# Filling a wait at a seam: eight early products, one transpose moved, and other shares of filler work

## The chip, the core and the metric

The kernel runs on one core of one Trainium2 chip. The metric is the device time of one execution in microseconds (us); lower is better. Matmuls run on TensorE (PE in the profile, with its weight loads as PEld), element-wise work on VectorE (DVE), exponentials and logarithms on ScalarE (ACT). GpSimd (POOL) and SyncE (SP) mainly start transfers here.

## The reference

Attention over 8 batches of 12 heads, with one extra term in the softmax's denominator, followed by a two-layer network with a squared ReLU over all 3584 tokens:

```python
batch, n_heads, seq, head_dim = (8, 12, 448, 64)
n_tokens, d_model, d_ff = (3584, 768, 2048)

scores = scale * q @ k.T
m = max(scores, axis=-1)
e = exp(scores - m)
attn = e / (sum(e) + exp(-m) + 1e-09)
x = (attn @ v)                 # heads side by side: 3584 x 768
h = x @ w_in                   # 768 x 2048
g = max(h, 0) ** 2
out = g @ w_out                # 2048 x 768, float32
```

The kernel leaves the maximum out of the exponent (sum(exp(s)) + 1 is the same denominator), so a head pair needs scores, exponentials, their sums, the products with v and one multiplication by the reciprocal.

## The kernel before

The order of the instructions on each engine is the order in which the program names them. Work is cut in units: one unit is one head pair of one batch, and unit number i is also the round of the loop that starts it. Batch 0 is cut twice: units 0 to 5 are its six head pairs for queries 0 to 191, units 6 to 11 the same pairs for queries 192 to 447. Units 12 to 17 are batch 1, 18 to 23 batch 2, and so on; from unit 18 on they run three to a cycle.

While a unit's exponentials run on ScalarE, TensorE is kept busy with products of the first layer, which are taken one at a time from a queue:

```python
def tile_in(t0, n, f0, per):          # one tile of the first layer: per * 6 products
    hp = mp_tile()                    # a PSUM tile: the pool m_psum has three
    for j in range(per):
        for dc in range(DCH):         # DCH = 6: the six head pairs are the contraction
            product(hp[...], win[...], xt[:, dc, x0:x0 + n], ...)
            yield n / 2.4             # nominal ns of a product of n columns
    relu_squared(hp, t0, n, f0, per)  # two VectorE instructions: rt, gs (they free hp)

def tiles_in_early(n, f0, per, ready):    # the first two tiles of batch 0
    hps = [mp_tile(), mp_tile()]
    for t, dcs in ((0, range(ready)), (1, range(ready)), (0, range(ready, DCH)), (1, range(ready, DCH))):
        ...     # first the 16 products that need only pairs 0 to 3, then the 8 that need pairs 4 and 5

def drain(ns):
    while ins and ns > 0:
        ns -= one(ins)                # one product; subtracts its nominal ns

def transposes(b, pr):                # q and k of one head pair: 16 transposes and a VectorE copy
    tp = mp_tile(FP16)
    ...                               # 16 x nc.tensor.transpose(tp[...], naturals[...], ident)
    nc.vector.tensor_copy(qks[b][...], tp[...])
```

A product is two matmuls of 64 columns of weights each. All tiles named mp (first layer, sums, transposes) come from the same three PSUM buffers; the values' tile xp has one buffer of its own. From the first cycle on every fourth mp tile takes xp's buffer.

```python
FIRST = 192
transpose_at = {pr - 1: [(0, pr)] for pr in range(1, NPAIR)}       # NPAIR = 6
for i, at in ((10, (1, 0)), (11, (1, 1)), (11, (1, 2)), (13, (1, 3)), (14, (1, 4)), (15, (1, 5)), (16, (2, 0)),
              (17, (2, 1)), (17, (2, 2))):
    transpose_at.setdefault(i, []).append(at)

for i in range(NPAIR, 2 * NPAIR):              # rounds 6 to 11
    u, et, es, half = begin(i)
    two = units[i - 2:i] if i % 2 == 0 else None    # even rounds sum and normalise two units
    if i % 2 or i == NPAIR:
        xp = x_psum.tile(...)
    scores(u, et, 0)                           # 4 matmuls, then one exponential of 112x1024
    if i == NPAIR:                             # the seam: round 6
        sums(i - 1)                            # VectorE: es of unit 5
        values_of(i - 2, xp)
        values_of(i - 1, xp)
        rcp = sums_of(i - 2)                   # TensorE: 4 matmuls; ScalarE: Ln, then Exp(-x)
        normalise(two, xp, rcp)                # VectorE: xt of pairs 4 and 5
        scores(u, et, 1)
        queue(0, FIRST)                        # 8 tiles of 12 products
        share[0] = left() / (NPAIR + 4)
    else:
        for at in transpose_at.get(i, ()):
            transposes(*at)
        drain(16 * FIRST / 2.4 if i == NPAIR + 1 else share[0] * 0.45)
        scores(u, et, 1)
        values_of(i - 1, xp)
        if two:
            rcp = sums_of(i - 2)
        drain(share[0] * 0.3)
    add_chunks(u, et, es, half, 1)             # VectorE: half
    if two and i > NPAIR:
        normalise(two, xp, rcp)
    add_chunks(u, et, es, half, 2)             # VectorE: es
    if i > NPAIR:
        drain(share[0] * 0.25)

for i in range(2 * NPAIR, 3 * NPAIR):          # rounds 12 to 17 (batch 1)
    ...
    scores(u, et, 0)
    for at in transpose_at.get(i, ()):
        transposes(*at)
    drain(share[0] * (1.2 if first else 0.45))
    scores(u, et, 1)
    ...                                        # round 12: values, sums; later rounds: sums, values of unit i - 1
    drain(share[0] * 0.15)
    for step in range(3):
        add_chunks(u, et, es, half, step)      # VectorE: es, half, es
        drain(share[0] * (0.15, 0.1, 0.15)[step])
    if i == 3 * NPAIR - 1:
        run(ins, len(ins))
        rcps[i] = row_sums([u], ...)           # sums of unit 17
    normalise(done, xp, rcp)
    if first:
        queue(FIRST, S - FIRST)                # 8 tiles of 12 products of 256 columns
        share[0] = left() / (NPAIR - 0.2)

for i in range(3 * NPAIR, NU, 3):              # the cycles
    for j in range(3):
        begin(i + j)
        for kk in range(RUN):
            scores(units[i + j], ets[i + j], kk // 2, (kk % 2,))
            ...                                # VectorE sums
            if (j, kk) != (2, RUN - 1):
                rows(5 if (RUN * j + kk) % 3 == 0 else 4)   # second layer: 4 or 5 steps of two matmuls
    ...
    if b in ON_PE and pr == 0:
        for x in range(3):
            transposes(b, 3 + x)
```

Of the kernel before, what the change touches and what calls it, by code (L numbers as in the profile page):

```python
# [15 lines left out]
def kernel(  # L16
# [14 lines left out]
    NPAIR = H // 2  # L31
# [121 lines left out]
    def transposes(b, pr):  # L153
        tp = mp_tile(FP16)
        for i, name in enumerate("qk"):
            for s in range(RUN):
                for h in range(2):
                    nc.tensor.transpose(tp[64 * h:64 * h + 64, i, P * s:P * s + P],  # L158
                                        naturals[name, b, pr][:, h, s, :], ident[0:P, 0:P])
        if b not in qks:  # L160
            qks[b] = qk_pool.tile([128, 3, COLS], FP16, name="qk")
        parts = (0, S // 2, S) if b == 0 and pr < 3 else (0, S)
        for x, y in zip(parts, parts[1:]):
            nc.vector.tensor_copy(qks[b][:, 0:2, pr * S + x:pr * S + y], tp[:, :, x:y])  # L164
# [67 lines left out]
    def values(u, et, xp, o=0):  # L232
        b, pr, _, n = u
        for kk in range(RUN):
            for h in range(2):
                nc.tensor.matmul(xp[64 * h:64 * h + 64, o:o + n], vns[b][:, 2 * pr + h, kk, :],  # L236
                                 of_head(chunk(et, u, kk // 2, kk), u, h), start=(kk == 0), stop=(kk == RUN - 1))

    def row_sums(us, sums):

        n = us[0][3]
        m = n * len(us)
        zp = mp_tile()
        for j, (u, parts) in enumerate(zip(us, sums)):
            for x, es in enumerate(parts):
                total = es[:, 0:2 * n]
                if n < S:
                    total = total.rearrange("p (h n) -> p h n", h=2)
                for h in range(2):
                    nc.tensor.matmul(zp[64 * h:64 * h + 64, j * n:(j + 1) * n], ones, of_head(total, u, h),  # L250
                                     start=(x == 0), stop=(x == len(parts) - 1))
        rcp = z_pool.tile([128, 512], FP32, name="rcp")
        nc.scalar.activation(out=rcp[:, 0:m], in_=zp[:, 0:m], func=AF.Ln, bias=one_b)  # L253
        nc.scalar.activation(out=rcp[:, 0:m], in_=rcp[:, 0:m], func=AF.Exp, scale=-1.0)  # L254
        return rcp
# [14 lines left out]
    def mp_tile(dtype=FP32):  # L270
        if joined[0] >= 0:
            joined[0] += 1
        pool, name = (x_psum, "xp") if joined[0] > 0 and joined[0] % 4 == 0 else (m_psum, "mp")
        return pool.tile([128, 512] if dtype == FP32 else [128, 2, 512], dtype, name=name)
# [22 lines left out]
    def tile_in(t0, n, f0, per):  # L297

        xt, x0 = xts[t0 // S], t0 % S
        hp = mp_tile()  # L300
        for j in range(per):
            fb = f0 + j
            for dc in range(DCH):
                product(hp[:, j * n:(j + 1) * n], win[:, dc, fb * 128:(fb + 1) * 128],
                        xt[:, dc, x0:x0 + n], start=(dc == 0), stop=(dc == DCH - 1))
                if j < per - 1 or dc < DCH - 1:
                    yield n / 2.4
        relu_squared(hp, t0, n, f0, per)
        yield n / 2.4

    def tiles_in_early(n, f0, per, ready):

        xt = xts[0]
        m = per * n
# [3 lines that stand above are left out]
                fb = f0 + per * t + j  # L318
                for dc in dcs:
                    product(hps[t][:, j * n:(j + 1) * n], win[:, dc, fb * 128:(fb + 1) * 128],  # L320
                            xt[:, dc, 0:n], start=(dc == 0 and j == 0), stop=(dc == DCH - 1 and j == per - 1))
                    if dc < DCH - 1 or j < per - 1:
                        yield n / 2.4
            if dcs[-1] == DCH - 1:
                relu_squared(hps[t], 0, n, f0 + per * t, per)
                yield n / 2.4
# [71 lines left out]
    def queue(t0, n):  # L398

        per = max(1, 512 // n)  # L400
        first = 0
        if t0 + n == FIRST:
            first = 2 * per
            ns = first * DCH * n / 2.4
            ins.append([ns, ns, tiles_in_early(n, 0, per, DCH - 2)])
        for f0 in range(first, NFFB, per):
            ns = per * DCH * n / 2.4
            ins.append([ns, ns, tile_in(t0, n, f0, per)])
# [10 lines left out]
    def left():  # L419
        return sum(t[0] for t in ins)  # L420

    def one(tiles):

        got = next(tiles[0][2])
        tiles[0][0] -= got
        if tiles[0][0] < 1.0:
            tiles.pop(0)
        return got

    def drain(ns):  # L430
        while ins and ns > 0:
            ns -= one(ins)
# [6 lines left out]
    FIRST = 192  # L439
# [3 lines left out]

    transpose_at = {pr - 1: [(0, pr)] for pr in range(1, NPAIR)}
    for i, at in ((10, (1, 0)), (11, (1, 1)), (11, (1, 2)), (13, (1, 3)), (14, (1, 4)), (15, (1, 5)), (16, (2, 0)),
                  (17, (2, 1)), (17, (2, 2))):
        transpose_at.setdefault(i, []).append(at)

    def keep_warm(n):
# [4 lines left out]
    share = [0.0]  # L454
# [25 lines left out]
    def sums_of(at):  # L480
        return row_sums(units[at:at + 2], (ess.pop(at)[0:1], ess.pop(at + 1)[0:1]))

    def values_of(at, xp):
        values(units[at], ets.pop(at), xp, at % 2 * units[at][3])
# [38 lines left out]
    for i in range(NPAIR, 2 * NPAIR):  # L523
        u, et, es, half = begin(i)
        two = units[i - 2:i] if i % 2 == 0 else None
        if i % 2 or i == NPAIR:
            xp = x_psum.tile([128, 512], FP32, name="xp")
        mode[0] = COLS2
        scores(u, et, 0)
        if i == NPAIR:  # L530
            sums(i - 1)
            values_of(i - 2, xp)
            values_of(i - 1, xp)
            rcp = sums_of(i - 2)
            normalise(two, xp, rcp)
            scores(u, et, 1)
            queue(0, FIRST)
            share[0] = left() / (NPAIR + 4)
        else:
            for at in transpose_at.get(i, ()):  # L540
                transposes(*at)
            drain(16 * FIRST / 2.4 if i == NPAIR + 1 else share[0] * 0.45)
            scores(u, et, 1)
            values_of(i - 1, xp)
            if two:
                rcp = sums_of(i - 2)
            drain(share[0] * 0.3)
        add_chunks(u, et, es, half, 1)
        if two and i > NPAIR:
            normalise(two, xp, rcp)  # L550
        add_chunks(u, et, es, half, 2)
        if i > NPAIR:
            drain(share[0] * 0.25)
        if i == NPAIR + 5:
            load_natural(2, 0, 3)
            for n0 in (0, HALF):
                for j in range(2):
                    load_wout(n0, j, 2)
# [56 lines left out]
    def add(at, *steps):  # L615
        for step in steps:
            add_chunks(units[at], ets[at], *ess[at], step)
# [5 lines left out]
    for i in range(3 * NPAIR, NU, 3):  # L623
        b, pr = units[i][0:2]
# [4 lines that stand above are left out]
                if kk == 0 and j:  # L629
                    add(i + j - 1, 1, 2)  # L630
                if kk == 1:
                    add(i + j, 0)
                if (j, kk) != (2, RUN - 1):
                    rows(5 if (RUN * j + kk) % 3 == 0 else 4)
        mode[0] = COLS2
        for at in pending:
            take_in(at)
# [3 lines that stand above are left out]
        if pr == 0:  # L641
            queue((b - 1) * S, S)
            if b > 2:
                run(outs)
            if b + 1 < B:
                transposed_loads(b + 1)
                hold(b + 1)
                load_v(b + 1, 0, NPAIR)
                if b + 2 < B:
                    stage(b + 2)  # L650

        run(ins, 1 if pr == 0 else 2)
        add(i + 2, 1)
        run(ins, 1)
        add(i + 2, 2)
        sum_up(i, i + 1)
        run(ins, 2)
        sum_up(i + 2)
        run(ins, 3 if pr == 0 else 4)
        if pr:  # L660
            complete(b * S)
        pending = [i, i + 1, i + 2]
# [36 lines left out]
```

The softmax here doesn't subtract the row's maximum and nothing guards it: scores larger than these inputs give would overflow.

## Time and profile before

| What | Value |
|---|---|
| time, median of 3 runs | 412.65 us (412.32 to 413.08) |
| span of the profiled execution | 410.6 us |
| granted TensorE clock | 0.999 |
| VectorE busy over the span | 289.8 us (71%) |
| ScalarE busy over the span | 234.4 us (57%) |
| TensorE busy, 10 to 20 us | 8.73 us of 10 |
| TensorE busy, 20 to 30 us | 9.18 us of 10 |
| TensorE busy, 65 to 70 us | 3.75 us of 5 |
| TensorE busy, 80 to 140 us | 60 us of 60 |

The span can be read in stages from the starts of the scores on TensorE: rounds 0 to 5 fill the first 17.7 us, round 6 begins at 17.70 us, round 12 at 35.87, round 17 at 59.86, and the first cycle at 67.5 us. [...] consecutive matmuls overlap in the record: what a group costs TensorE is read from the start of the group to the start of the next, not from its duration.

### The profile page before, as it was taken

The numbers are of one execution on the slowest core, as the hardware profiler recorded it, in microseconds if no ns is written. First come the engines' busy times: TensorE is split into PE (matmuls) and PEld (weight loads), VectorE is DVE, ScalarE is ACT, GpSimd is POOL, SyncE is SP. The second block draws the span as 40 slices with busy tenths as digits, with TensorE's granted clock in tenths as the row PEclk, the third lists the DMA queues.
The fourth block names the chain that finished last, engine by engine and source line by source line (L and its number), as shares of the span: only waits on it lengthen the run. The fifth ranks groups of instructions, "written<-read, shape, count | busy, mean of one in ns | idle before, by whom it ended". The sixth has DMA issues, their size and how long they took to land.

```text
span 410.6 us, 10685 instructions
## 1 busy us (share of the span) xinstructions
PE 401.0 (98%) x4715; PEld 259.0 (63%) x4715; DVE 289.8 (71%) x554; ACT 234.4 (57%) x312; POOL 36.3 (9%) x58
## 2 busy tenths in 40 slices
PE   7899998999999999999999999999999999999997
PEld 3577676755576666666566666667566665555664
DVE  3778896978976787777876788867876789186000
ACT  5998997667393745559383755739464663100111
POOL 7524030020000200001000030001000000000000
PEclk9999999999999999999999999999999999999999
DMA  9999999689114891499304992297102010010222
GB/s 203 197 198 197 203 202 219 127 132 219 60 42 107 135 219 25 98 183 182 100 2 114 168 179 64 77 188 124 41 2 69 11 41 2 38 40 0 78 77 78
DMA packets 75823, 45.58 MB, mean 111 GB/s; under 512 B 42560, under 2 KB 72000, under 8 KB 75456
## 3 DMA queue, kind: packets, MB, share of 16 engines
q0 software_dynamic: 28848, 22.16, 35.6%
q1 hardware_dynamic: 46208, 22.05, 23.1%
q8 instruction: 37, 0.61, 0.6%
q10 hardware_dynamic: 720, 0.69, 0.5%
q14 instruction: 10, 0.08, 0.1%
HBM read 45.69 MB, written 17.93 MB: 155 GB/s over the span
## 4 chain that ended last, share of the span: by engine, by line
PE 89%; ACT 4%; DVE 4%; DMA 1%; issue 1%
PE mp L286 24%; PE mp L352 17%; PE mp L288 11%; PE xp L286 8%; PE sp L201 6%; PE xp L352 5%; PE mp L236 5%; PE xp L288 3%; PE xp L236 3%; PE sp L189 3%; ACT et L169 3%; PE mp L250 2%; PE mp L158 1%; DMA et<-in_k_dram 1%; DVE qk L164 1%; ACT rcp L253 1%
## 5 line engine op out<-in xcount | busy, mean ns | idle before, releaser
L169 ACT ACTIVATE et<-sp 112x896 f16<-112x896 f32 (+2 forms) x144 | 125.2, 915 | 40.7 <-PE sp L201 30.6
L352 PE MATMUL mp<-wout,gs 64*128 64x384 f16 x896 | 115.2, 322 | 0.0
L286 PEld LDWEIGHTS <-win 128*64 128x64 f16 x1536 | 83.9, 110 | 45.6 <-issue 1.5
L286 PE MATMUL mp<-xt,win 128*64 128x448 f16 (+2 forms) x1200 | 107.0, 323 | 0.3 <-DVE qk L164 0.2
L293 DVE TENSOR_SCALAR rt<-mp 128x448 f16<-128x448 f32 (+2 forms) x96 | 59.7, 622 | 26.3 <-PE mp L286 13.8
L352 PEld LDWEIGHTS <-gs 64*128 64x128 f16 x1152 | 58.1, 94 | 21.1
L295 DVE TENSOR_TENSOR gs<-rt 128x448 f16<-128x448 f16 (+2 forms) x128 | 50.2, 392 | 4.4
L352 PE MATMUL xp<-wout,gs 64*128 64x384 f16 x256 | 53.1, 323 | 0.0
L253 ACT ACTIVATE rcp<-mp,one_b 128x448 f32<-128x448 f32 (+2 forms) x42 | 26.5, 630 | 41.9 <-PE mp L250 41.7
L361 ACT ACTIVATE ot<-mp 128x384 f32<-128x384 f32 (+1 forms) x16 | 7.6, 477 | 64.5 <-PE mp L288 48.2
L201 PE MATMUL sp<-qk 64*112 64x224 f16 x480 | 43.1, 258 | 0.0
L169 ACT ACTIVATE nn<-sp 112x896 f16<-112x896 f32 x48 | 41.7, 917 | 1.6
L201 PEld LDWEIGHTS <-qk 64*112 64x112 f16 x480 | 30.6, 128 | 14.2 <-issue 3.6
L286 PE MATMUL xp<-xt,win 128*64 128x448 f16 x336 | 36.5, 352 | 0.0
L288 PEld LDWEIGHTS <-gs 128*128 128x128 f16 x256 | 24.4, 98 | 15.1 <-issue 0.4
L236 PEld LDWEIGHTS <-vn 112*64 112x64 f16 x432 | 22.4, 109 | 15.4 <-issue 3.9
L288 PE MATMUL mp<-wout,gs 128*128 128x384 f16 (+1 forms) x192 | 30.3, 317 | 0.0
L214 DVE TENSOR_TENSOR es<-et 112x896 f16<-112x896 f16 x30 | 18.7, 623 | 15.8 <-ACT et L169 15.3
L254 ACT ACTIVATE rcp<-rcp 128x448 f32<-128x448 f32 (+2 forms) x48 | 27.7, 577 | 1.5
L189 PE MATMUL sp<-qk 64*112 64x448 f16 (+2 forms) x192 | 25.8, 320 | 1.4 <-ACT et L169 0.6
L216 DVE TENSOR_TENSOR es<-es,half 112x896 f16<-112x896 f16 x42 | 26.2, 623 | 1.0
L293 DVE TENSOR_SCALAR rt<-xp 128x448 f16<-128x448 f32 x32 | 19.9, 622 | 8.2 <-PE xp L286 6.7
(63 smaller groups left out, 340.0 us busy)
## 6 DMA issues: line engine op xcount, KB each, us to landing
vn<-in_v_dram POOLq DMA_DIRECT2D x7, 672.0 KB, 9.0
out_dram<-ot SPq DMA_DIRECT2D x9, 384.0 KB, 2.3
win<-in_moe_w_in_dram POOLq DMA_DIRECT2D x8, 384.0 KB, 14.2
wout<-in_moe_w_out_dram POOLq DMA_DIRECT2D x4, 768.0 KB, 18.0
stage_q<-in_q_dram POOLq DMA_DIRECT2D x4, 676.0 KB, 11.3
stage_k<-in_k_dram POOLq DMA_DIRECT2D x4, 676.0 KB, 14.7
out_dram<-ot SPq DMA_DIRECT2D x8, 288.0 KB, 9.0
out_dram<-ot SPq DMA_DIRECT2D x9, 192.0 KB, 2.7
```

Of the source, the lines that this page charges most:

```text
L169: nc.scalar.activation(out=out_, in_=in_, func=AF.Exp, scale=scale)
L189: nc.tensor.matmul(sp[:, h, o:o + n], qk[r, 1, x + P * kk:x + P * kk + P], qk[r, 0, x + q0:x + q0 + n], start=True, stop=True)
L201: nc.tensor.matmul(sp[:, odd, h * (S // 2):(h + 1) * (S // 2)], qk[r, which, kx:kx + 2 * P - 1:2], qk[r, 0, x:x + S // 2], start=True, sto ...
L216: nc.vector.tensor_add(es, es, half[:, 0:2 * S])
L236: nc.tensor.matmul(xp[64 * h:64 * h + 64, o:o + n], vns[b][:, 2 * pr + h, kk, :], of_head(chunk(et, u, kk // 2, kk), u, h), start=(kk == 0 ...
L253: nc.scalar.activation(out=rcp[:, 0:m], in_=zp[:, 0:m], func=AF.Ln, bias=one_b)
L254: nc.scalar.activation(out=rcp[:, 0:m], in_=rcp[:, 0:m], func=AF.Exp, scale=-1.0)
L286: nc.tensor.matmul(out_[x:x + 64], lhsT[:, x:x + 64], rhs, start=start, stop=stop)
L288: nc.tensor.matmul(out_, lhsT, rhs, start=start, stop=stop)
L293: nc.vector.tensor_scalar(out=rt[:, 0:m], in0=hp[:, 0:m], scalar1=0.0, scalar2=None, op0=ALU.max)
L295: nc.vector.tensor_mul(gs[:, f0:f0 + per, t0 % RING:t0 % RING + n], r, r)
L352: nc.tensor.matmul(o[:, 0:w], g[x:x + 64], wout[x:x + 64, fb, n0:n0 + w], start=(fb == 0), stop=(fb == NFFB - 1))
```

## The change

The first part puts eight products of the queue ahead of the sums of units 4 and 5 in round 6. The sums of unit 5 are still being added up on VectorE at that time, and these eight products need only pairs 0 to 3, which are normalised. Round 7 gets 14 products in place of 16 before its second scores. The second part gives the odd rounds of batch 0 other shares of filler: more of it ahead of the values, less behind them. The third takes the transpose of pair 2 of batch 2 out of round 17, which had two of them, and puts it into the first cycle, after the third scores of unit 18.

```diff
-                  (17, (2, 1)), (17, (2, 2))):
+                  (17, (2, 1))):
...
             values_of(i - 1, xp)
+            queue(0, FIRST)
+            share[0] = left() / (NPAIR + 4)
+            drain(8 * FIRST / 2.4)
             rcp = sums_of(i - 2)
             normalise(two, xp, rcp)
             scores(u, et, 1)
-            queue(0, FIRST)
-            share[0] = left() / (NPAIR + 4)
         else:
             for at in transpose_at.get(i, ()):
                 transposes(*at)
-            drain(16 * FIRST / 2.4 if i == NPAIR + 1 else share[0] * 0.45)
+            drain(14 * FIRST / 2.4 if i == NPAIR + 1 else share[0] * (0.45 if two else 0.7))
             scores(u, et, 1)
             values_of(i - 1, xp)
             if two:
                 rcp = sums_of(i - 2)
-            drain(share[0] * 0.3)
+            drain(share[0] * (0.3 if two else 0.1))
         ...
         if i > NPAIR:
-            drain(share[0] * 0.25)
+            drain(share[0] * (0.25 if two else 0.2))
...
                 if kk == 1:
                     add(i + j, 0)
+                if (i, j, kk) == (3 * NPAIR, 0, 2):
+                    transposes(2, 2)
                 if (j, kk) != (2, RUN - 1):
                     rows(5 if (RUN * j + kk) % 3 == 0 else 4)
```

## The prediction

> **What bounds the kernel now.** I read the page's first rows, then TensorE's waits, then the timelines of the rounds that the change touches.
>
> ```profile
> PE 401.0 (98%) x4715; PEld 259.0 (63%) x4715; DVE 289.8 (71%) x554; ACT 234.4 (57%) x312; POOL 36.3 (9%) x58
> ...
> PE mp L250 <- DVE es L216: 1.1, 1, 1.1
> PE sp L189 <- ACT et L169: 0.6, 2, 0.4
> PE xp L236 <- DVE xt L265: 0.4, 1, 0.4
> PE mp L286 <- DVE qk L164: 0.2, 1, 0.2
> PE mp L250 <- DVE qk L164: 0.2, 1, 0.2
> PE mp L250 <- DVE rt L293: 0.2, 1, 0.2
> PE mp L250 <- DVE es L221: 0.2, 1, 0.2
> ```
>
> TensorE is the bound, and from 20 to 80 us it has only small named waits (total, times, longest): 2.9 us in all. From 80 us to 140 us it has none. The change takes no work away, so it can win only part of these waits. The longest is before the sums of unit 17 (1.1 us, round 17). The second view is TensorE's timeline at the seam, where the end of es of unit 5 holds the sums:
>
> ```profile
> 18.98 0.85 PE L236 MATMUL xp<-et,vn 112*64 112x192 f16 x16 [0.86 <-DVE xt L265]
> 19.64 0.28 PE L250 MATMUL mp<-es,ones 112*64 112x192 f16 x2
> 20.07 0.27 PE L250 MATMUL mp<-es,ones 112*64 112x192 f16 x2 [0.16 <-DVE es L221]
> 20.28 0.64 PE L189 MATMUL sp<-qk 64*112 64x256 f16 x8
> 20.85 1.51 PE L286 MATMUL mp<-xt,win 128*64 128x192 f16 x32
> 22.48 0.42 PE L189 MATMUL sp<-qk 64*112 64x256 f16 x4
> ...
> 20.39 0.58 ACT L253 ACTIVATE rcp<-mp,one_b 128x384 f32<-128x384 f32 x1 [0.43 <-PE mp L250]
> 21.00 0.53 ACT L254 ACTIVATE rcp<-rcp 128x384 f32<-128x384 f32 x1
> 21.43 4.87 ACT L169 ACTIVATE et<-sp 112x1024 f16<-112x1024 f32 x5
> ```
>
> ScalarE waits at 20.39 and is then solid to 26.30: here it is ScalarE's chain that paces the rounds. The third view is round 11, TensorE and VectorE:
>
> ```profile
> 33.67 0.58 PE L286 MATMUL mp<-xt,win 128*64 128x192 f16 x10
> 34.18 0.42 PE L189 MATMUL sp<-qk 64*112 64x256 f16 x4
> 34.54 0.63 PE L236 MATMUL xp<-et,vn 112*64 112x256 f16 x8
> 35.25 0.69 PE L286 MATMUL mp<-xt,win 128*64 128x192 f16 x12
> ...
> 34.58 1.15 DVE L164 COPY qk<-mp 128x896 f16<-128x896 f16 x2
> ```
>
> The values cost 0.46 us from start to start in round 7 (22.84 to 23.30), so TensorE is through with them at 35.0 and the next products wait to 35.25: until the first of the two copies ends, 34.58 + 0.57. The products open a new tile, and it takes the buffer that the first transpose left. This wait is under the list's threshold, and the change works on it.
>
> **What the Trainium skill says.** Perfetto Trace Analysis, Identifying the Most-Contended Engine, says that matmul busy share is a poor measure because pipelined matmuls overlap; so it is here (98% busy, weight loads 63%), and I use start-to-start times. The same page, Identifying Performance Opportunities, says that a repeating bubble can mean that there is no PSUM for the next tile. The wait at 35.0 is such a one, if a single one. PSUM — Partial Sum Buffer, Engine vs sequencer instructions, says that VectorE's queue is strictly first in, first out, and that matmuls start in program order. The trace agrees: nothing overtakes the products at 35.25. TensorE: Matmul & The Clock Gate, Part 4, says that a transpose lands in PSUM and needs a VectorE copy; here 16 transposes take 0.41 us (29.95 to 30.36) and the copy 0.62.
>
> **The change part by part.** A product of 192 columns costs 0.093 us: 24 matmuls from 36.38 to 37.49 are 12 products in 1.11. Changes of tile add about 0.06 per group.
>
> *Round 6 and 7.* The eight products go from 19.64 to about 20.42, and es of unit 5 is ready at 20.02, so the sums then run through: TensorE wins the 0.2 us. But ScalarE's rcp, which waits for the sums, starts 0.45 later, at 20.84 in place of 20.39, and its Exp ends at 21.98; xt of pairs 4 and 5 follows at 22.00 to 22.56. Scores (0.57) and eight more products bring TensorE from 20.62 to 21.94. The last six of the 14 need pairs 4 and 5: they wait to 22.61, 0.66 us. Second scores of round 7: 22.61 + 0.62 = 23.23 against 22.48. The wait is moved, and ScalarE is 0.45 late.
>
> *Rounds 8 to 10.* Products done at the end of round 7: 8 + 14 + 1 + 2 = 25, against 22 (the shares are 9.6 products; each drain rounds up). In round 9 seven products stand ahead of the values in place of five, and three behind in place of six. The values there wait for xt behind the rcp: 28.54 + 0.45 = 28.99. The shorter tail brings round 10 to 28.99 + 0.46 + 0.33 = 29.8 against 29.59, and round 11 to about 32.75 against 32.51.
>
> *Round 11.* 57 products are done when it starts; tiles have 12, so three are left of the fifth tile. The odd round now asks for seven ahead of the second scores: the other four open the sixth tile, while the two transposes hold two of the three buffers and the fifth tile the third. The new tile must wait for the first copy. On VectorE the copy stands behind xt of units 8 and 9, which waits for their rcp (33.60 before, some 0.25 later now), and es: it ends at 35.15 + 0.25 = 35.4. TensorE is there at 32.75 + 0.36 + 0.81 + 0.31 = 34.2, so it waits 1.2 us where 0.25 was. Behind it follow four products (0.43), scores (0.36), values (0.46), three products (0.34): round 12 begins at 37.05 against 35.87, **1.2 us late**. Products done: 67 against 66, worth 0.1. Round 12 opens a stretch in which ScalarE had no gap (36.30 to 44.12), so nothing is made up.
>
> *Batch 1.* Ten products of 192 are left after round 12 in place of eleven, so round 13 starts its 256-column tiles one product earlier, and in rounds 14 and 17 a tile now ends in the drain ahead of the first sum in place of behind it. VectorE then waits for that tile before es, and es (0.65) comes behind rt and gs. In round 14 VectorE idled 0.80 before that rt; without es in front it idles about 1.4, and the copy of round 15 comes some 0.6 late (52.7 for 52.1). The sums there already waited for it (the 0.2 of the list). Counted through, round 17 begins about 0.7 late.
>
> *Round 17.* One transpose less: 0.41, and the wait of 0.22 for its buffer goes. VectorE loses one copy. Second scores come 0.8 earlier, but es is again behind rt and gs of the tile: from the tile's end, rt 0.72, gs 0.35, es, half and es three times 0.65, then the sums. Worked through without the 0.7, the sums come at 66.83 for 67.21: 0.38 won. Round 14 and 17 together: 0.3 to 0.4 lost.
>
> *First cycle.* TensorE pays the 0.41 of the transpose here; from 70.57 on its scores follow each other at 0.84 and 1.00, its own pace, so it is paid in full. The second pair of the second layer's tiles now takes the transpose's buffer and may wait 0.15 for the copy, which stands behind es of unit 18 (70.52 to 71.14). Together 0.5.
>
> Sum: 1.2 + 0.35 + 0.5 = 2.0 us on 412.65, or 414.7. I take 414.0, since three of the terms are counted by hand through 40 us, and each has a way out.
>
> **Rivals.** *The filler works as meant*: the waits of 0.2 at 20.07, 0.42 at 28.54, part of the 1.13 at 67.21 go, and the new tile of round 11 finds a buffer. The gain is then up to 1.0 us: 411.7 to 412.3. For it: ScalarE's gap at 20.39 and the wait at 28.54 are there. Against it: the buffers of round 11 can be counted, and in round 11 the copy cannot be earlier than 35.15 unless rcp is. *Only the seam counts*: round 11's wait is there but batch 1 absorbs half of it, since VectorE's order shift does not reach TensorE: 413.0 to 413.5. *ScalarE bounds all of rounds 6 to 13*: then the 0.45 at the rcp is the whole loss, 413.1. *VectorE becomes the bound in batch 1* (it is solid from 49.31 to 62): the order shift grows to over 1 us, 415 and more.
>
> **Range and chances.** The low end, 412.4, holds the case in which the waits won pay for those made; the high end, 415.2, holds the sum with 0.5 more. 2% are 8.2 us, and no wait here is of that size, so "within 2%" is nearly certain.
>
> **What would show it.** Right: in the changed trace the products of round 7 wait about 0.6 for xt (the line of normalise), those of round 11 over 1 us for qk (the copy), round 12 begins near 37 us, and the sums of unit 17 still wait over 1 us for es. Wrong: round 12 begins before 35.9, or no wait for qk in round 11; then the buffers were not as I count them. If round 12 is at 37 but round 17 is not later than that, the reading of VectorE's order in batch 1 fails. If the first cycle, from the sums of unit 17 to its first first-layer products, is not longer than before (67.21 to 80.06), the transpose has been hidden.

## The result and the profile after

The changed kernel takes 414.22 us (median of 4, 414.12 to 414.67) against 412.80 for the kernel before in the same comparison (412.32 to 413.08). The ratio is 1.0038, with an interval of 1.002 to 1.0055: slower by a third of a percent, inside the predicted range and 0.2 us from the predicted 414.0. The profiled span grew from 410.6 to 412.4 us.

The page's first row of the changed kernel, and its list of TensorE's waits from 20 to 80 us (who waited for whom: total, times, longest):

```profile
PE 401.2 (97%) x4715; PEld 257.5 (62%) x4715; DVE 289.7 (70%) x554; ACT 234.7 (57%) x312; POOL 35.9 (9%) x58
...
PE mp L250 <- DVE es L216: 1.7, 1, 1.7
PE mp L286 <- DVE qk L164: 1.2, 1, 1.2
PE mp L250 <- DVE qk L164: 0.6, 1, 0.6
PE mp L286 <- DVE xt L265: 0.5, 1, 0.5
PE xp L236 <- DVE xt L265: 0.4, 1, 0.4
PE sp L189 <- ACT et L169: 0.4, 1, 0.4
```

The work is the same: 4715 matmuls and 554 VectorE instructions in both. The list was 2.9 us and is 4.8. The wait for es of unit 5 is gone, which was the purpose; each of the first four lines is a wait that was absent or smaller before. The timelines place them. The seam and round 11, TensorE and then the two copies on VectorE:

```profile
20.36 0.36 PE L250 MATMUL mp<-es,ones 112*64 112x192 f16 x4
...
21.22 0.85 PE L286 MATMUL mp<-xt,win 128*64 128x192 f16 x16
22.53 0.69 PE L286 MATMUL mp<-xt,win 128*64 128x192 f16 x12 [0.46 <-DVE xt L265]
...
33.62 0.42 PE L286 MATMUL mp<-xt,win 128*64 128x192 f16 x6
35.20 0.52 PE L286 MATMUL mp<-xt,win 128*64 128x192 f16 x8 [1.16 <-DVE qk L164]
35.66 0.42 PE L189 MATMUL sp<-qk 64*112 64x256 f16 x4
...
34.53 1.15 DVE L164 COPY qk<-mp 128x896 f16<-128x896 f16 x2
```

In the seam the sums run through (four in one group), and the wait has moved behind the 16 products that need no new xt. In round 11 three products (6 matmuls) finish a tile; the fourth opens the next one and starts at 35.20, just after the first of the two copies (34.53 + 0.62; the two overlap a little in the record and last 1.15 together). The second scores, which ScalarE needs, stand behind it.

Starts read from the timelines give the time of each stage, in us. Differences within one profile are used, since each profile enters round 6 at a slightly different time (17.67 to 17.99).

| Stage, from start to start | before | changed | difference |
|---|---|---|---|
| round 6 to round 12 | 18.17 | 19.07 | +0.90 |
| round 12 to round 17 | 23.99 | 24.62 | +0.63 |
| round 17 to the sums of unit 17 | 7.35 | 6.98 | -0.37 |
| these sums to the cycle's first products of 448 columns | 12.85 | 13.47 | +0.62 |
| all four | 62.36 | 64.14 | +1.78 |

The two spans differ by the same 1.8, and what lies ahead of round 6 and behind the last stage differs by under 0.1, so the time is lost in these four stages. The medians differ by less, 1.42, but the kernel before had 412.80 from 4 executions there; in two larger sets below, of 40 and 32, it had 412.57.

### The profile page after: what moved, and what is told of

Same layout as the page of the kernel before. It is cut to its first block, busy times and chain, and to the rows that moved or that the text cites. A ratio compares the mean times of both kernels' runs of the same rounds, so it can differ in the third digit from the quotient of the medians.

```text
span 412.4 us, 10683 instructions
## 1 busy us (share of the span) xinstructions
PE 401.2 (97%) x4715; PEld 257.5 (62%) x4715; DVE 289.7 (70%) x554; ACT 234.7 (57%) x312; POOL 35.9 (9%) x58
## 4 chain that ended last, share of the span: by engine, by line
PE 90%; ACT 4%; DVE 3%; DMA 1%; issue 0%; ACTq 0%
PE mp L286 24%; PE mp L352 17%; PE mp L288 10%; PE xp L286 8%; PE sp L201 6%; PE mp L236 5%; PE xp L352 5%; PE xp L288 4%; PE xp L236 4%; PE sp L189 3%; ACT et L169 2%; PE mp L250 2%; PE mp L158 1%; DMA et<-in_k_dram 1%; ACT rcp L254 1%; ACT rcp L253 1%
## 5 line engine op out<-in xcount | busy, mean ns | idle before, releaser
L286 PE MATMUL mp<-xt,win 128*64 128x448 f16 (+2 forms) x1236 | 110.6, 323 | 1.6 <-DVE qk L164 1.2
L293 DVE TENSOR_SCALAR rt<-mp 128x448 f16<-128x448 f32 (+2 forms) x99 | 61.5, 622 | 29.8 <-PE mp L286 17.4
L352 PEld LDWEIGHTS <-gs 64*128 64x128 f16 x1152 | 56.3, 94 | 22.6
L352 PE MATMUL xp<-wout,gs 64*128 64x384 f16 x288 | 59.3, 322 | 0.0
L253 ACT ACTIVATE rcp<-mp,one_b 128x448 f32<-128x448 f32 (+2 forms) x40 | 25.3, 632 | 42.4 <-PE mp L250 42.4
L361 ACT ACTIVATE ot<-mp 128x384 f32<-128x384 f32 (+2 forms) x15 | 7.1, 470 | 59.3 <-PE mp L288 47.0
L286 PE MATMUL xp<-xt,win 128*64 128x448 f16 x300 | 32.5, 352 | 0.0
L288 PE MATMUL mp<-wout,gs 128*128 128x384 f16 (+2 forms) x192 | 29.6, 313 | 0.0
L359 DVE TENSOR_SCALAR ot<-mp 128x384 f32<-128x384 f32 x28 | 15.6, 558 | 9.8 <-PE mp L352 5.9
```

What stands on the lines that cost most here:

```text
L286: nc.tensor.matmul(out_[x:x + 64], lhsT[:, x:x + 64], rhs, start=start, stop=stop)
L288: nc.tensor.matmul(out_, lhsT, rhs, start=start, stop=stop)
L293: nc.vector.tensor_scalar(out=rt[:, 0:m], in0=hp[:, 0:m], scalar1=0.0, scalar2=None, op0=ALU.max)
L352: nc.tensor.matmul(o[:, 0:w], g[x:x + 64], wout[x:x + 64, fb, n0:n0 + w], start=(fb == 0), stop=(fb == NFFB - 1))
```

## The experiments

Each was timed (5 to 17 executions) beside the kernel before, which had medians of 412.57, 412.57 and 412.79 in the three sets. Differences are to the kernel before of the same set unless another is named. First, each part alone on the kernel before; the number of products done at the start of every later round is kept, except where that number is the question.

**The seam alone.** The eight early products and 14 in round 7, none later in round 7, so that 22 are done at its end as before.

```diff
+            queue(0, FIRST)
+            share[0] = left() / (NPAIR + 4)
+            drain(8 * FIRST / 2.4)
             rcp = sums_of(i - 2)
...
-            drain(16 * FIRST / 2.4 if ...)
+            drain(14 * FIRST / 2.4 if ...)
...                                   # the two later drains only for i > NPAIR + 1
```

> The kernel before with the early products of the seam alone (8 in round 6, 14 in round 7, none later in round 7, so that every later round starts with the same number of products done as before). Theory A (the wait is only moved, and ScalarE's rcp is 0.4 us later): a wait of 0.4 to 0.7 us for xt in round 7, round 8 starts 0.1 to 0.5 us later, round 12 starts within 0.2 us of 35.87, time within 0.3 us of before. Theory B (the seam is what made the changed kernel slower): round 12 starts near 36.8, time 1.0 us up. Theory C (the filler works as meant): round 12 near 35.6, time 0.2 us down or better.

Measured: 412.43 us, ratio 0.9996 (0.9988 to 1.0004). The stage from round 6 to 12 took 18.06 (18.17 before), the others are as before to 0.01. TensorE has the same new wait at the end of the same work:

```profile
22.65 0.69 PE L286 MATMUL mp<-xt,win 128*64 128x192 f16 x12 [0.46 <-DVE xt L265]
```

Theory A's wait is there, and the time moves by less than 0.3 us. The filler takes the wait away and hands it on; what remains is 0.1 us in one profile, and the time does not resolve it. Theory B fails. Theory C is not excluded by the time, whose interval reaches 0.5 us down, but the stage shows 0.11 won where it needed about 0.3. This run also tests whether a late rcp is carried on. Measured from the start of round 6, the rcp of that round starts 0.31 later than before (20.87 - 17.87 against 20.39 - 17.70), and that of round 8 starts 0.11 earlier (26.47 - 17.87 against 26.41 - 17.70): the delay is gone after two rounds.

**Round 11's shares alone.** 11 products as before, in the order 7, 1, 3 in place of 5, 3, 3.

```diff
-            drain(... share[0] * 0.45)
+            drain(... share[0] * (0.7 if i == 2 * NPAIR - 1 else 0.45))
...
-            drain(share[0] * 0.3)
+            drain(share[0] * (0.1 if i == 2 * NPAIR - 1 else 0.3))
```

> The kernel before with other shares in round 11 alone: 7 products ahead of the second scores, 1 behind the values, 3 at the end, 11 in all as before. Theory A (the sixth tile has no buffer until the first copy ends): TensorE waits about 1.2 us for the copy there, round 12 starts 0.8 to 1.0 us later (36.7 to 36.9), time 0.8 to 1.0 us up. Theory B (the order of 11 products in one round does not matter to TensorE): round 12 at 35.9, time as before.

Measured: 413.61 us, ratio 1.0023 (1.0015 to 1.0032), 1.04 up. TensorE in round 11:

```profile
33.94 0.58 PE L286 MATMUL mp<-xt,win 128*64 128x192 f16 x10
35.52 0.36 PE L286 MATMUL mp<-xt,win 128*64 128x192 f16 x4 [1.00 <-DVE qk L164]
35.80 0.42 PE L189 MATMUL sp<-qk 64*112 64x256 f16 x4
```

Five products finish the tile, the sixth waits. The stage to round 12 took 19.09 (+0.92), and the stage behind it 24.10 (+0.11). Two products moved across the scores cost 1 us: theory A.

**One product more, and nothing else**, at the end of round 11.

```diff
-            drain(share[0] * 0.25)
+            drain(share[0] * (0.35 if i == 2 * NPAIR - 1 else 0.25))
```

> The kernel before with one product more at the end of round 11, so that one less is left and the wide tiles of batch 1 start one product earlier. Theory A (a tile that ends ahead of the first sum puts es behind rt on VectorE): the wait of the sums in round 15 for the copy grows from 0.20 to about 0.6 us, the sums of unit 17 come 0.4 to 0.7 us later than before, time 0.4 to 0.7 us up. Theory B (one product of 0.09 us moved is worth no more than itself): time within 0.15 us.

Measured: 413.18 us, ratio 1.0014 (1.0006 to 1.0022), 0.61 up, from 0.09 us of work done early. VectorE in round 14, first in the kernel before, then in this run, and TensorE's wait in round 15 of this run:

```profile
47.89 0.62 DVE L214 TENSOR_TENSOR es<-et 112x896 f16<-112x896 f16 x1
49.31 0.69 DVE L293 TENSOR_SCALAR rt<-mp 128x512 f16<-128x512 f32 x1 [0.80 <-PE mp L286]
...
49.59 0.69 DVE L293 TENSOR_SCALAR rt<-mp 128x512 f16<-128x512 f32 x1 [1.65 <-PE mp L286]
50.31 0.43 DVE L295 TENSOR_TENSOR gs<-rt 128x512 f16<-128x512 f16 x1
50.65 0.62 DVE L214 TENSOR_TENSOR es<-et 112x896 f16<-112x896 f16 x1
...
53.59 0.38 PE L250 MATMUL mp<-es,ones 112*64 112x448 f16 x2 [0.63 <-DVE qk L164]
```

VectorE sits idle for 1.65 us ahead of rt, and only then does the first es. In the kernel before that es ran at 47.89 in the idle time, and the idle was 0.80. The stage from round 12 to 17 took 24.43 (+0.44). In round 17 the same order made the wait ahead of the sums 1.67, but that stage as a whole took only 0.06 more: the wait of 0.22 for the buffer is gone there, and the second scores come 0.36 earlier. Theory A; the product itself is not what costs.

**The transpose alone** moved from round 17 into the first cycle.

```diff
-                  (17, (2, 1)), (17, (2, 2))):
+                  (17, (2, 1))):
...
+                if (i, j, kk) == (3 * NPAIR, 0, 2):
+                    transposes(2, 2)
```

> The kernel before with the transpose of pair 2 of batch 2 moved from round 17 into the first cycle, and nothing else. Theory A: the wait for the buffer in round 17 (0.22) and 0.41 of transposes go, the sums of unit 17 come 0.8 us earlier (66.4), the cycle pays 0.4 to 0.7; time 0.1 to 0.4 us down. Theory B (the 1.1 us wait ahead of the sums just grows by what round 17 wins, and the cycle pays in full): time 0.4 to 0.7 us up.

Measured: 412.47 us, ratio 0.9996 (0.9988 to 1.0004). Round 17 to its sums took 6.56 (-0.79), the stretch behind it 13.47 (+0.62). TensorE in the cycle, the third and fourth scores of the kernel before and then this run:

```profile
69.73 0.40 PE L189 MATMUL sp<-qk 64*112 64x448 f16 x2
70.57 0.40 PE L189 MATMUL sp<-qk 64*112 64x448 f16 x2
...
68.92 0.40 PE L189 MATMUL sp<-qk 64*112 64x448 f16 x2
69.25 0.58 PE L158 MATMUL mp<-ident,nn 112*64 112x112 f16 x16
69.76 0.82 PE L352 MATMUL mp<-wout,gs 64*128 64x384 f16 x8
70.42 0.35 PE L189 MATMUL sp<-qk 64*112 64x448 f16 x2
```

From scores to scores it is 1.50, where the kernel before took 0.84 for the same scores and steps (69.73 to 70.57): the transpose costs 0.66 here. The stages fit theory A, at its lower end: won 0.79, paid 0.62. The time alone does not resolve a gain, but it excludes theory B, and the wait ahead of the sums stayed at 1.13.

The four differences, -0.14, +1.04, +0.61 and -0.10, add up to +1.41; the change measured +1.42. That agreement is luck, for the stages do not add up so:

| Stage | the four parts together | changed kernel |
|---|---|---|
| round 6 to round 12 | +0.88 | +0.90 |
| round 12 to round 17 | +0.56 | +0.63 |
| round 17 to the sums of unit 17 | -0.74 | -0.37 |
| these sums to the first products of 448 columns | +0.62 | +0.62 |
| all four | +1.32 | +1.78 |

Three stages add up to within 0.1. In round 17 two parts win the same time: from its start to its second scores the kernel before takes 2.81, the one product more 2.45, the moved transpose 2.01, and the changed kernel, which has both, also 2.01. The wait that the order costs behind these scores, 0.42, stays in full. The other shares of rounds 7 and 9 were not run alone; that the first stage adds up leaves little room for them.

**The changed kernel with round 11 fitted to the tile**: its ten products as 3, 4, 3.

```diff
-            drain(... share[0] * (0.45 if two else 0.7))
+            drain(... share[0] * (0.45 if two else 0.3 if i == 2 * NPAIR - 1 else 0.7))
...                                   # and 0.4 and 0.25 in that round's later drains
```

> The changed kernel with round 11's ten products split 3, 4, 3 in place of 7, 1, 2, so that no new tile is opened ahead of the second scores. Theory A (the missing buffer costs the changed kernel about 1 us): the wait of 1.16 us for the copy goes down to under 0.5 behind the values, round 12 starts 0.8 to 1.0 us earlier than in the changed kernel (35.8 to 36.0), time 0.8 to 1.0 us below it, at 413.2 to 413.4. Theory B (the rest of the change carries the loss): time within 0.3 us of the changed kernel.

Measured: 413.36 us, against the kernel before 1.0019 (1.0011 to 1.0026), 0.79 up where the changed kernel was 1.42 up. The medians themselves differ by 0.86, but across two sets; the stages differ by 1.11. The stage to round 12 took 18.15 again, and the next 24.42. So the missing buffer is worth 0.92 in its own stage and 0.20 in the one behind it. The rest of the loss stays in this run: +0.43 in batch 1 by the order on VectorE, -0.36 in round 17, where a transpose less and the order meet, and +0.62 in the first cycle.

**The second transpose of round 11 at the round's end**, in the changed kernel, and one product less there (7, 1, 1), so that 66 are done as before.

```diff
-    for i, at in ((10, (1, 0)), (11, (1, 1)), (11, (1, 2)), ...
+    for i, at in ((10, (1, 0)), (11, (1, 1)), ...
...
-            drain(share[0] * (0.25 if two else 0.2))
+            drain(share[0] * (0.25 if two else 0.1 if i == 2 * NPAIR - 1 else 0.2))
+        if i == 2 * NPAIR - 1:
+            transposes(1, 2)
```

> The changed kernel with the second transpose of round 11 put at the round's end, so that only one buffer is held while the sixth tile opens, and one product less in that round (7, 1, 1; 66 done, as in the kernel before). Theory A: no wait for the copy in round 11, round 12 starts 0.2 to 0.5 us earlier than in the kernel before (35.4 to 35.7), the sums of round 15 wait 0.2 again, time 0.3 to 0.7 us below the kernel before (411.9 to 412.3). Theory B (the copies on VectorE come no earlier, and another wait takes the place): time within 0.2 us of the kernel before.

Measured: 412.14 us, ratio 0.9992 (0.9984 to 1.0), 0.43 below the kernel before; by the four stages it is 2.2 below the changed one. TensorE in round 11 has no wait left:

```profile
32.74 0.58 PE L158 MATMUL mp<-ident,nn 112*64 112x112 f16 x16
33.16 0.75 PE L286 MATMUL mp<-xt,win 128*64 128x192 f16 x14
33.83 0.42 PE L189 MATMUL sp<-qk 64*112 64x256 f16 x4
```

Seven products cross from one tile to the next in 0.67. The stages are 17.96 (-0.21), 23.99 (0), 6.56 (-0.79) and 13.47 (+0.62). With one transpose between, a buffer is free when the tile opens, and with 66 products done the order in batch 1 is the old one. The last two stages are those of the moved transpose, which this run keeps.

**The sums of unit 17 later**, on the kernel before: behind the third scores of unit 18, and round 17's last products ahead of half and es.

```diff
             drain(share[0] * (0.15, 0.1, 0.15)[step])
-        if i == 3 * NPAIR - 1:
-            run(ins, len(ins))
-            rcps[i] = row_sums([u], (ess.pop(i)[0:1],))
+            if i == 3 * NPAIR - 1:
+                run(ins, len(ins))
...
+                if (i, j, kk) == (3 * NPAIR, 0, 2):
+                    sum_up(3 * NPAIR - 1)
```

> The kernel before with the sums of unit 17 taken out of the end of round 17 and put behind the third scores of unit 18, and with the last products of round 17 ahead of half and es. Theory A (the 1.1 us wait ahead of these sums is a wait of the order, which scores and second-layer steps of unit 18 can fill): the wait goes, the first second-layer steps start 0.8 to 1.4 us earlier, the transposes behind the cycle's scores come 0.7 to 1.2 us earlier, time 0.7 to 1.2 us down. Theory B (ScalarE, which does twelve exponentials and a reciprocal in that stretch, bounds it): the wait turns into one of scores for ScalarE, time less than 0.4 us down.

Measured: 411.64 us, ratio 0.9975 (0.9965 to 0.9985). Round 17 to the cycle's first products of 448 columns took 19.08 in place of 20.20. Of the wait of 1.13 a rest of 0.27 stays, at the new place:

```profile
68.31 0.35 PE L189 MATMUL sp<-qk 64*112 64x448 f16 x2
68.94 0.38 PE L250 MATMUL mp<-es,ones 112*64 112x448 f16 x2 [0.27 <-DVE es L216]
```

The scores of unit 18 and the second layer's steps between them now fill the time in which VectorE adds up es. ScalarE does not bound the stretch: theory A. In this profile rounds 6 to 12, which the edit does not touch, took 18.34; the 0.17 more is the first wait of round 6 for xt, 1.04 in place of 0.86, and no effect of the edit.

**Both edits** on the changed kernel, with the transpose of pair 2 back in round 17.

> The two edits together on the changed kernel (second transpose of round 11 at the round's end; sums of unit 17 behind the third scores of unit 18), with the transpose of pair 2 of batch 2 back in round 17. Theory A (the terms add): 1.0 to 1.7 us below the kernel before, 410.9 to 411.6. Theory B (ScalarE or VectorE becomes the bound once both waits are gone): no better than the better of the two alone.

Measured: 411.17 us, ratio 0.9968 (0.9956 to 0.9981): 1.40 below the kernel before. The stages are those of the two runs put together: 17.96, 23.99, and 19.08 from round 17 on. The terms add, and this version beats both kernels (5 executions).

**The transpose between round 17 and the cycle**, on that version, with the sums one scores group later.

```diff
-                  (17, (2, 1)), (17, (2, 2))):
+                  (17, (2, 1))):
...
+        if i == 3 * NPAIR - 1:            # behind the last products
+            transposes(2, 2)
...
-                if (i, j, kk) == (3 * NPAIR, 0, 2):
+                if (i, j, kk) == (3 * NPAIR, 0, 3):
                     sum_up(3 * NPAIR - 1)
```

> The kernel of the run before (both edits) with the transpose of pair 2 of batch 2 between the last products of round 17 and the scores of unit 18, and the sums of unit 17 behind the fourth scores of unit 18. Theory A (the 0.66 us that this transpose cost in the first cycle is 0.41 of transposes and 0.25 of standing among second-layer steps): here it costs 0.40 to 0.45 from its start to the scores, the buffer wait of 0.22 in round 17 goes, time 0.1 to 0.3 us below the run before. Theory B (16 transposes cost 0.66 wherever no other wait hides them): 0.6 to 0.7 from its start to the scores, time as the run before or 0.1 up.

Measured: 411.57 us, ratio 0.9971 (0.996 to 0.9983): no gain on the run before (1.22 below its own kernel before, where that one was 1.40 below). TensorE:

```profile
65.34 0.56 PE L158 MATMUL mp<-ident,nn 112*64 112x112 f16 x16
65.83 0.40 PE L189 MATMUL sp<-qk 64*112 64x448 f16 x2
...
70.66 0.32 PE L352 MATMUL mp<-wout,gs 64*128 64x384 f16 x1 [0.47 <-ACT rcp L253]
```

From the start of the transposes to the scores it is 0.49, between the two theories and outside both numbers. But part of that was there before: from the start of the last products to the scores of unit 18 it is 2.24 (63.59 to 65.83), against 1.84 in the run before (63.94 to 65.78), for the same 16 products. So the transposes add 0.40, as theory A had it, and not 0.66. The buffer wait of round 17 is gone, but a new one of 0.47 stands in the cycle: a second-layer tile waits until ScalarE has read a sum. From round 17 on this took 19.34, against 19.08 in the run before. I read it as an extra tile between two pairs of tiles, which shifts who inherits whose buffer; no run separates the moved sums from the moved transpose. The expected time was missed for a wait that I had not counted.

## Why the prediction was right

**Rounds 6 to 10: the mechanism right, the size too large.** I had the new wait for xt at 0.66; it is 0.46. I had ScalarE's rcp 0.45 late; it starts at 20.75 against 20.39, and 0.05 of that is the later start of the profile. I carried the 0.45 through the rounds, and that was the wrong step; the run of the seam alone shows it too (0.31 late in round 6, 0.11 early in round 8). In round 8 the sums of the kernel before waited 0.2 for rt, and ScalarE waited with them. In the changed kernel rt comes earlier and that wait is gone, so the next rcp is at 26.60 against 26.41, 0.14 late with the start of the profile taken off. Round 11 began at 32.46, not at 32.75; against 32.51 before, and with two products more done, the change was ahead there.

**Round 11: right.** Predicted wait 1.2, measured 1.16, for the named copy. Both of its ends came 0.2 to 0.3 earlier than I had put them, so the wait kept its size. (A copy lasts 0.62 here and not 0.57, and the terms to round 12 add up to 36.99 and not 37.05; both are small.) Round 12 was put 1.2 late and is 0.90 late; the 0.3 between is the term above. The single run of round 11's shares and the fitted run give +0.92 and -0.92.

**Batch 1: 0.7 predicted, 0.63 measured, of which 0.43 is what I had named.** The order of es behind rt gives 0.44 alone and 0.43 in the fitted run. That the total came near 0.7 is luck. The other 0.20 I did not have: it goes when round 11 is fitted, so it follows from that wait (0.11 where the shares of round 11 alone were changed). In round 13 of the changed kernel the transpose starts 0.72 behind the scores (40.71 to 41.43), where 0.52 was usual (39.76 to 40.28), and ScalarE ends the first half of an rcp, which reads the sums, at 40.69 + 0.69 = 41.38. The transposes start 0.05 behind that end in four profiles, though their distance from the scores differs: 40.23 and 40.28 before, 40.49 and 40.54 in the fitted run, 41.52 and 41.57 with the shares alone, 41.38 and 41.43 here. (Behind the copy in round 11 it is 0.05 too: 35.15 and 35.20.) So they most likely wait for the buffer of these sums, which come late because ScalarE stood idle in round 11; no run changes this alone.

**Round 17: right.** I had 0.38 won, and it is 0.37: -0.79 by the transpose that left, and 0.42 given back to the order of es, as I had worked it through (the wait ahead of the sums grew from 1.13 to 1.67).

**First cycle: the sum near, its parts wrong.** Predicted 0.41 for the transposes and 0.15 for the copy, together 0.5; measured 0.62. There is no wait for the copy; the transposes themselves cost 0.66 at that place.

**The sum.** By its terms it was 2.0; the stages show 1.78, and the medians 1.42, with an interval of the ratio that spans 0.8 to 2.3 us. The main miss is the 0.3 of rounds 6 to 10. The 414.0 was this sum less 0.7, taken off by judgement with no term named for it; that it fell 0.2 from the measured time is luck. Of the rivals, the one in which the filler works as meant fails in round 11; the seam alone does neither harm nor good that the time resolves, and batch 1 absorbs nothing of round 11's wait; ScalarE as the only bound fails, since the fitted run leaves 0.8 us of loss with round 12 on time. VectorE as the bound in batch 1 is half right: its order delays TensorE, but by 0.44 and not by over 1.

## What to carry to other kernels

Before filler is moved on an engine that keeps its order, count the tiles: a product that opens a new tile needs a buffer, and if the next one to come free hangs on an engine several steps behind, everything after that product waits too (1.16 us here). Work taken from a queue in fixed numbers has a phase: one product more or less decides whether the evacuation of a tile stands ahead of or behind a sum on VectorE, rounds later, and was worth far more than the product here (0.61 us for 0.09). Filler that leads to the next dependence only moved the wait at the seam; it helped where the waiting instruction itself can be put later, as with the sums of unit 17.

## What the runs showed of the hardware

Sixteen transposes of 112 columns add 0.41 us to TensorE's time between scores and products of the first layer (29.95 to 30.36 in the kernel before), 0.40 between products and scores (last run), and 0.66 among second-layer steps, which read 64 rows (scores to scores 1.50 for 0.84). The 0.25 more stands on both sides of the transposes. The first of them starts 0.33 behind the scores (68.92 to 69.25), where a second-layer step starts 0.19 behind them (69.73 to 69.92 in the kernel before); and from the first transpose to the next step it is 0.51 (69.25 to 69.76).

Neither side belongs to the transposes alone. Scores read 64 rows, and values, which read 112 rows as transposes do, also start 0.33 behind two scores (77.77 to 78.10 in the kernel before). And the 0.51 has its like in the last run, where scores follow the transposes: 0.49, of which only 0.40 is added time. So by these profiles a change from 64 rows to more costs about 0.14, and one back about 0.1; between first-layer scores and products both are paid with or without the transposes. That the number of rows is the reason fits these times and was not tried.
